# A two-layer expert network behind an attention: where the late weight conversions stand

## The chip, the cores and the metric
One core of a Trainium2 chip. The metric is the device time of one execution in microseconds (us), the median of several runs. TensorE does the matmuls (PE; its weight loads are shown as PEld), VectorE is DVE, ScalarE is ACT, GpSimd is POOL. SyncE (SP) issues all DMAs of this kernel, one after the other in program order.

## The reference, cut to what matters
All arithmetic is in float32; the matmuls have float32-like precision.

```
a     = softmax of phi (8, 8, 576, 32) over the 576 positions
k_m   = a^T k,  v_m = a^T v            # (8, 8, 32, 64): 32 memory slots per head
attn  = softmax(q k_m^T / 8)           # p: 576 x 32 per head
x     = attn v_m, heads side by side   # 4608 tokens x 512
h     = x @ w_in1;  g = h - tanh(h);   x = g @ w_out1      # 512 -> 2048 -> 512
h     = x @ w_in2;  g = h > 0 ? h : exp(min(h, 0)) - 1;  out = g @ w_out2
```

The four weight matrices arrive as 64-bit floats. The kernel turns them into float32 itself, and splits each value into a high and a low part, so that three matmuls (high x high, high x low, low x high) give a product of float32 precision.

## The kernel before, in words
A weight matrix is cut into 8 pages of 256 of the 2048 inner features. `conv` (L574) converts half a page: it loads 512 KB of raw words into one of three raw buffers (L580, L583), waits some rounds, and runs `convert` (L40): ACT takes an absolute value (L48), DVE does two tensor_scalars (L50, L51) and two scalar_tensor_tensors (L54, L57), ACT copies the high part (L62) and POOL subtracts it for the low part (L64). Pages 0 to 3 of the first layer's w_in stay whole (no split). For the second layer the two parts go to a staging tile and are stored to DRAM (L605); the first layer's parts stay on chip.

`Staged` (L251) spreads generators over rounds. `round` steps every live generator once, and starts a new one every second round, from the deque `first` and, if that is empty, from `todo`. `half` steps only those that asked for it: a conversion's ACT step (L48) is put there. `drain` runs rounds until nothing is left.

The first layer runs in 64 blocks (L765). A block is one slice `sw` of four (two pages, that is 512 inner features) by one group of 288 tokens `n`. `ss` is the half of the slices: blocks 0 to 31 hold slices 0 and 1 (pages 0 to 3), blocks 32 to 63 slices 2 and 3 (pages 4 to 7). For each of its two pages a block does `h_unit` (L349, 12 matmuls at L357: p against vw), the tanh-like function on ACT, POOL and DVE (`g_a` to `g_d`), and two `x_unit`s (L396, 12 matmuls each at L405) that lag behind by a block and more. `vw` is v_m times w_in, remade for each pair of batches (`vw_whole` at L344 for whole pages, `vw_half` at L328 for split ones). Units of attention (`units`) are stepped beside the blocks until the last one is done; then the pool of `at1` closes and its space goes to `wt3`, `vw2` and `wt2`.

In each block `cv.round()` is called once per page (L831), so that one conversion starts per block; in blocks 0 to 6 and 26 to 30 it is called a second time per page (L853, L854), so that two start. `need` (L568) runs further rounds at once where a page is wanted that is not converted.

Weight pages of the first layer lie in four pools. In `wt0` and `wt1`, on the right side of the memory, w_in pages use tags wi0 and wi1 (one 8 KB tile with a high and a low half per partition; pages 0 to 3 use only the first half) and w_out pages 0 to 3 use wo0 and wo1. Pages 4 and 5 of w_in take the tiles of pages 0 and 1, pages 6 and 7 those of 2 and 3. w_out pages 4, 5 are in `wt2`, pages 6, 7 in `wt3`; both pools exist only after `at1` closes. The pages 4 to 7 are converted from block 24 on: w_in 4, 5 are put in front at block 24, w_out 4, 5 behind them when `at1` closes, w_in 6, 7 and w_out 6, 7 at block 28. The second layer's 32 conversions are in `todo` from block 15.

At block 60 `open_l2` (L706) drains the conversions, closes `wt1` and `wt0` and opens the second layer's pools in their place; its first x loads (`load_x`, L434, into three xr buffers), sums (`add_x`, L440) and weight loads (L721) are then issued in blocks 60 to 63 by the list `soon`. `wt2` is closed at block 62. The second layer follows (L466 and L508).

Of the kernel before, what the change touches and what calls it, by code (L numbers as in the profile page):

```python
# [8 lines left out]
F32 = mybir.dt.float32  # L9
F32R = mybir.dt.float32r  # L10
# [15 lines left out]
NSW = 4  # L26
# [265 lines left out]
class Moe1:  # L292
# [23 lines left out]
    def vw_half(self, vm, wi, pg, po):  # L316
        nc = self.nc
        pars = range(2)
        if po == 0:
            for par in pars:  # L320
                pool = self.vw2_p if self.vw2_p and par and pg // 2 % 2 else self.vw_p
                self.vw[par, pg] = [pool.tile([128, 2, 256], F32R, tag=f"vw{pg % 2}_{par}{t}", name="vw")
                                    for t in range(2)]
        ps = self.misc.tile([128, 2, 256], F32, tag="m", name="vw_ps")
        for kc in range(2):
            p = 2 * po + kc
            for i, (a, b) in enumerate(((0, 0), (0, 1), (1, 0))):
                nc.tensor.matmul(ps[:, kc], lhsT=vm[:, a, p, :], rhs=wi[:, b, p, :], start=(i == 0), stop=(i == 2))  # L328
        parts = [(ps[64 * par:64 * par + 64], *(t[64 * po:64 * po + 64] for t in self.vw[par, pg])) for par in pars]
        for src, hi, lo in parts:  # L330
            nc.scalar.activation(hi, src, ACTF.Copy)
        for src, hi, lo in parts:
            nc.vector.tensor_tensor(lo, src, r32(hi), op=ALU.subtract)  # L333

    def vw_whole(self, vm, wi, pg, par, slot):
        nc = self.nc
        pool = self.vw2_p if self.vw2_p and par and pg // 2 % 2 else self.vw_p
        hi, lo = self.vw[par, pg] = [pool.tile([128, 2, 256], F32R, tag=f"vw{pg % 2}_{slot}{t}", name="vw")
                                     for t in range(2)]
        ps = self.misc.tile([128, 2, 256], F32, tag="m", name="vw_ps")  # L340
        for kc in range(2):
            for po in range(2):
                p = 2 * po + kc
                nc.tensor.matmul(ps[64 * po:64 * po + 64, kc], lhsT=vm[:, p, 64 * par:64 * par + 64],  # L344
                                 rhs=wi[:, 0, p, :], start=True, stop=True)
        nc.scalar.activation(hi, ps, ACTF.Copy)
        nc.vector.tensor_tensor(lo, ps, r32(hi), op=ALU.subtract)

# [47 lines left out]
    def x_unit(self, sw, n, dm, wo, on_act):  # L396
        nc = self.nc
        ps = self.misc.tile([128, NB], F32, tag="m", name="x_ps")
        k = 0
        for i in range(2):  # L400
            pg = 2 * sw + i
            g = self.g[n, pg]
            for j in range(2):
                for a, b in ((0, 0), (1, 0), (0, 1)):
                    nc.tensor.matmul(ps, lhsT=wo[pg][:, a, j, 128 * dm:128 * dm + 128], rhs=g[:, b, j, :],  # L405
                                     start=(k == 0), stop=(k == 11))
                    k += 1
        if dm % 2 == 0:
            self.x2[sw, n, dm // 2] = self.x_p.tile([128, 2, NB], F32, tag="x", name="x")
        t = self.x2[sw, n, dm // 2]  # L410
        if on_act:
            nc.scalar.activation(t[:, dm % 2], ps, ACTF.Copy)  # L412
        else:
            nc.vector.tensor_copy(t[:, dm % 2], ps)
        if dm == 3:
            for i in range(2):
                del self.g[n, 2 * sw + i]
# [113 lines left out]
def moe_kernel(tc, q, k, v, phi, w1, w2, w3, w4, out):  # L531
    nc = tc.nc
    with ExitStack() as top, tc.manual_schedule():
# [12 lines left out]
        wt_p = {0: new(l1b, "wt0", 1, side="right")}  # L546
# [8 lines left out]
        vm, vms = {}, {}  # L555
# [6 lines left out]
            return vm[b // 2][:, 2 * g:2 * g + 2, 64 * (b % 2):64 * (b % 2) + 64]  # L562

        wi, wo = {}, {}
        part = lambda t, h, c: t[:, h].rearrange("p a f -> p (a f)")[:, 512 * c:512 * c + 512]
        converted = set()

        def need(kind, pg, with_units=False):  # L568
# [5 lines left out]
        def conv(layer, kind, pg, c, lead=2):  # L574

            w = {("i", 1): w1, ("o", 1): w2, ("i", 2): w3, ("o", 2): w4}[kind, layer]
            raw = raw_p.tile([128, 512], mybir.dt.int64, tag="raw", name="raw")
            if kind == "i":
                src = w.rearrange("(k p) f -> p k f", p=128)[:, 2 * c:2 * c + 2, 256 * pg:256 * pg + 256]
                nc.sync.dma_start(out=raw.rearrange("p (a f) -> p a f", a=2), in_=src)  # L580
            else:
                r0 = 256 * pg + 128 * c
                nc.sync.dma_start(out=raw, in_=w[r0:r0 + 128, :])  # L583
            for k in range(lead + 1):
                yield k == lead
            staged, whole = [], (layer, kind) == (1, "i") and pg < 4

            def dst():
                if layer == 1:
                    ws = wi if kind == "i" else wo  # L590
                    if c == 0:
                        pool = wt_p[pg // 2 % (2 if kind == "i" else NSW)]
                        shape = [128, 2, 4, 256] if kind == "i" else [128, 2, 2, 512]
                        ws[pg] = pool.tile(shape, F32 if whole else F32R, tag=f"w{kind}{pg % 2}", name="w1")
                    if whole:
                        return part(ws[pg], 0, c)
                    return part(ws[pg], 0, c), part(ws[pg], 1, c)
                staged.append(wst_p[0].tile([128, 2, 512], F32R, tag="wst", name="wst"))
                return staged[-1][:, 0], staged[-1][:, 1]

            yield from convert(nc, cv_p, cv_ps, raw, dst, whole)
            converted.add((layer, kind, pg, c))
            if layer == 2:
                yield
                nc.sync.dma_start(out=w_dram[kind][pg, :, :, 512 * c:512 * c + 512], in_=r32(staged[-1]))  # L605

        conv_pair = lambda layer, kind, pg: [conv(layer, kind, pg, c) for c in range(2)]
        conv_l1 = lambda kind, *pgs: [g for pg in pgs for g in conv_pair(1, kind, pg)]
# [13 lines left out]
        cv = Staged([conv(1, "i", 1, 1)] + conv_l1("o", 0, 1), 2)  # L622
# [142 lines left out]
        for bi, (ss, bp, sub, j) in enumerate(blocks):  # L765
# [30 lines left out]
            if at1_open and 2 * B - 1 in p_done:  # L796
                at1_ctx.close()
                at1_open = False
                wt_p[3] = new(l1c, "wt3", 1)
                m1.vw2_p = new(l1c, "vw2", 1)  # L800
                wt_p[2] = new(late_ctx, "wt2", 1)
                cv.first.extend(conv_l1("o", 4, 5))
            if bi == 15:
                cv.todo.extend(conv_l2)
            if bi == 24:
                cv.first.extendleft(reversed(conv_l1("i", 4, 5)))
            if bi == 28:
                cv.first.extend(conv_l1("i", 6, 7) + conv_l1("o", 6, 7))
            if ss == 1 and j == 0 and sub == 1 and bp + 1 < B // 2 or bi == 28:
                load_vm((bp + 1) % (B // 2))  # L810
                vm_split = (bi + 1, (bp + 1) % (B // 2))
# [2 lines left out]
            for i in range(2):  # L814
                pg = 2 * sw + i
# [34 lines left out]
                x_next(bi < 22)  # L850
                m1.g_c(n, pg)
                cv.half()
                if bi < 7 or 26 <= bi < 31:  # L853
                    cv.round()  # L854
                    cv.half()
                units.round()
# [66 lines left out]
```

## Time and profile before
| | |
|---|---|
| median of 3 runs | 1709.38 us (1705.76 to 1710.95) |
| profiled execution | 1713.89 us, of it 1712.1 span |
| PE busy | 1613.9 us, 94% of the span |
| VectorE, ScalarE, GpSimd busy | 1187.0 us (69%), 931.0 us (54%), 757.2 us (44%) |
| granted TensorE clock, mean | 0.971 |

The span is the time from the first to the last instruction that the profile shows. Busy shares are means over stages that have different limits: the first layer ends at about 894 us, and behind it PE is hardly ever idle. A granted clock of 1.00 is 2.4 GHz and 0.5 is 1.2 GHz.

### The profile page before, as it was taken

The numbers are of one execution on the slowest core, as the hardware profiler recorded it, in microseconds if no ns is written. First come the engines' busy times: TensorE is split into PE (matmuls) and PEld (weight loads), VectorE is DVE, ScalarE is ACT, GpSimd is POOL, SyncE is SP. The second block draws the span as 40 slices with busy tenths as digits, with TensorE's granted clock in tenths as the row PEclk, the third lists the DMA queues.
The fourth block names the chain that finished last, engine by engine and source line by source line (L and its number), as shares of the span: only waits on it lengthen the run. The fifth ranks groups of instructions, "written<-read, shape, count | busy, mean of one in ns | idle before, by whom it ended". The sixth has DMA issues, their size and how long they took to land.

```text
span 1712.1 us, 26572 instructions
## 1 busy us (share of the span) xinstructions
PE 1613.9 (94%) x9884; PEld 1394.7 (81%) x9884; DVE 1187.0 (69%) x1730; ACT 931.0 (54%) x1677; POOL 757.2 (44%) x540
## 2 busy tenths in 40 slices
PE   5578999999989999999989999999999999999998
PEld 3346888787888999999989988888888888888886
DVE  4776767677989999999865655556555655565654
ACT  2455767677778888889853333333333333333332
POOL 1145655566666776767742222222222222222222
PEclk8668999999999999999999999999999999999999
DMA  8756566566565556666579321212121212121000
GB/s 194 213 172 179 176 188 198 182 201 226 192 212 176 170 193 219 220 214 215 182 238 360 103 62 48 74 49 63 49 74 42 70 50 74 50 65 59 25 14 25
DMA packets 140921, 236.09 MB, mean 138 GB/s; under 512 B 8184, under 2 KB 102392, under 8 KB 138744
## 3 DMA queue, kind: packets, MB, share of 16 engines
q1 hardware_dynamic: 140792, 234.39, 42.9%
q8 instruction: 78, 1.28, 0.3%
q14 instruction: 51, 0.42, 0.1%
HBM read 158.73 MB, written 74.45 MB: 136 GB/s over the span
## 4 chain that ended last, share of the span: by engine, by line
PE 65%; DVE 4%; DMA 4%; ACT 2%; issue 2%; POOL 1%; DVEq 0%; ACTq 0%; SPq 0%; POOLq 0%
PE h_ps L466 23%; PE o_ps L508 23%; PE x_ps L405 11%; PE h_ps L357 6%; PE vw_ps L328 1%; DMA p<-p_dram 1%; DMA xr<-x_dram 1%; DMA x_dram<-x 1%; DMA raw<-in_moe_w_in_dram 1%; DVE s L385 1%; DVE vw L333 1%; DVE h_ps L384 1%; ACT t L368 0%; DVE s L386 0%; POOL g L393 0%
## 5 line engine op out<-in xcount | busy, mean ns | idle before, releaser
L405 PE MATMUL x_ps<-g,w 128*128 128x288 f32 x3072 | 442.5, 297 | 11.8 <-POOL w L64 4.7
L492 POOL TENSOR_TENSOR e<-hm,e 128x512 fp32r<-128x512 f32 x144 | 187.1, 1299 | 576.9 <-ACT e L491 529.2
L405 PEld LDWEIGHTS x_ps<-g,w 128*128 128x128 f32 x3072 | 418.6, 189 | 25.6 <-ACT x L412 6.5
L466 PE MATMUL h_ps<-x,wi 128*128 128x512 f32 (+1 forms) x1920 | 424.6, 371 | 0.0
L508 PE MATMUL o_ps<-wo,e 128*128 128x512 f32 x1728 | 422.8, 393 | 0.7 <-POOL e L492 0.7
L466 PEld LDWEIGHTS h_ps<-x,wi 128*128 128x128 f32 x1920 | 336.1, 188 | 68.0
L508 PEld LDWEIGHTS o_ps<-wo,e 128*128 128x128 f32 x1728 | 323.4, 188 | 75.3 <-POOL e L492 1.1
L477 ACT ACTIVATE t_ps<-hm 128x512 f32<-128x512 f32 x144 | 86.7, 602 | 505.7 <-DVE hm L476 505.7
L375 POOL TENSOR_TENSOR v<-t,u 128x576 f32<-128x576 f32 x128 | 183.6, 1434 | 177.9 <-ACT u L369 161.1
L357 PE MATMUL h_ps<-p,vw 128*128 128x288 f32 x1536 | 240.2, 307 | 12.6 <-DVE s L386 6.6
L357 PEld LDWEIGHTS h_ps<-p,vw 128*128 128x128 f32 x1536 | 219.2, 196 | 24.5 <-issue 20.5
L483 DVE SCALAR_TENSOR_TENSOR hm<-hm,t_ps 128x512 f32<-128x512 f32 x144 | 99.1, 688 | 200.3 <-ACT hm L478 200.3
L393 POOL TENSOR_TENSOR g<-s,g 128x576 fp32r<-128x576 f32 x128 | 199.0, 1555 | 78.8 <-ACT g L392 71.5
L476 DVE TENSOR_SCALAR hm<-h_ps 128x512 f32<-128x512 f32 x144 | 99.6, 692 | 129.9 <-PE h_ps L466 129.2
L385 DVE SCALAR_TENSOR_TENSOR s<-s,v 128x576 f32<-128x576 f32 x128 | 137.3, 1073 | 7.3 <-POOL v L375 7.2
L368 ACT ACTIVATE t<-h_ps 128x576 f32<-128x576 f32 x128 | 83.3, 651 | 91.1 <-PE h_ps L357 38.8
L386 DVE COPY_PREDICATED s<-big,h_ps 128x576 f32<-128x576 uint32 x128 | 106.6, 833 | 12.8 <-ACT x L412 0.5
L370 ACT ACTIVATE s<-u,bias 128x576 f32<-128x576 f32 x128 | 99.5, 778 | 25.1 <-POOL g L393 15.5
L484 DVE SCALAR_TENSOR_TENSOR hm<-hm,t_ps 128x512 f32<-128x512 f32 x144 | 99.0, 688 | 5.0
L485 DVE TENSOR_TENSOR hm<-hm,h_ps 128x512 f32<-128x512 f32 x144 | 98.9, 687 | 5.0
L384 DVE TENSOR_TENSOR h_ps<-h_ps,t 128x576 f32<-128x576 f32 x128 | 96.6, 755 | 2.8 <-ACT u L369 2.7
L478 ACT ACTIVATE hm<-hm 128x512 f32<-128x512 f32 x144 | 91.0, 632 | 13.1
(88 smaller groups left out, 1681.2 us busy)
## 6 DMA issues: line engine op xcount, KB each, us to landing
x_dram<-x SPq DMA_DIRECT2D x128, 288.0 KB
xr<-x_dram SPq DMA_DIRECT2D x72, 512.0 KB
p<-p_dram SPq DMA_DIRECT2D x62, 576.0 KB
raw<-in_moe_w_in_dram SPq DMA_DIRECT2D x32, 512.0 KB
raw<-in_moe_w_out_dram SPq DMA_DIRECT2D x32, 512.0 KB
w_dram<-wst SPq DMA_DIRECT2D x32, 512.0 KB
kv<-in_k_dram SPq DMA_DIRECT2D x16, 576.0 KB
kv<-in_v_dram SPq DMA_DIRECT2D x16, 576.0 KB
```

The source lines that it names most:

```text
L357: nc.tensor.matmul(ps[:, j, :NB], lhsT=vw[a][:, kc, 128 * j:128 * j + 128], rhs=p[:, kc, b, :], start=(k == 0), stop=(k == 5))
L370: nc.scalar.activation(s, u, ACTF.Square, bias=bias[:, 0:1], scale=G_S)
L375: nc.gpsimd.tensor_tensor(v, t, u, op=ALU.mult)
L384: nc.vector.tensor_tensor(d, d, t, op=ALU.subtract)
L385: nc.vector.scalar_tensor_tensor(s, s, G_B, v, op0=ALU.add, op1=ALU.mult)
L386: nc.vector.copy_predicated(s, big.bitcast(U32), d)
L393: nc.gpsimd.tensor_tensor(g[:, 1], s, r32(g[:, 0]), op=ALU.subtract)
L405: nc.tensor.matmul(ps, lhsT=wo[pg][:, a, j, 128 * dm:128 * dm + 128], rhs=g[:, b, j, :], start=(k == 0), stop=(k == 11))
L466: nc.tensor.matmul(out, lhsT=w3[:, a, kc, 128 * j:128 * j + 128], rhs=x[:, b, kc, :], start=(i == 0), stop=(i == 11))
L476: nc.vector.tensor_scalar(hm, w[0], 0.0, None, op0=ALU.min)
L492: nc.gpsimd.tensor_tensor(e[:, 1], hm, r32(e[:, 0]), op=ALU.subtract)
L508: nc.tensor.matmul(acc, lhsT=e[:, a, jj, 128 * tg:128 * tg + 128], rhs=w4[:, b, j, :], start=(k == 0 and jj == 0 and i == 0), stop=(k == l ...
```

## The change
The tiles of the first layer's weights become halves of 4 KB per partition, and the halves that the whole w_in pages left unused get a tag of their own. The high parts of w_in pages 4 to 7 still take the places of pages 0 to 3; their low parts go to `wt2`. w_out page 4 goes to the two spare halves in `wt0` (tags wi0b, wi1b), page 5 to those in `wt1`; pages 6, 7 stay in `wt3`. So w_out 4, 5 no longer have to wait for `at1` to close: they are put into `todo` at block 8. The second layer's conversions are put there at block 12. When `at1` closes, w_out 6, 7 are put into `first`; at block 28 w_in 6, 7 go in front of them. The second call of `cv.round()` in blocks 26 to 30 goes away.

```
-                nc.tensor.matmul(ps[:, kc], lhsT=vm[:, a, p, :], rhs=wi[:, b, p, :], start=(i == 0), stop=(i == 2))
+                nc.tensor.matmul(ps[:, kc], lhsT=vm[:, a, p, :], rhs=wi[b][:, p, :], start=(i == 0), stop=(i == 2))
...
                     if c == 0:
-                        pool = wt_p[pg // 2 % (2 if kind == "i" else NSW)]
-                        shape = [128, 2, 4, 256] if kind == "i" else [128, 2, 2, 512]
-                        ws[pg] = pool.tile(shape, F32 if whole else F32R, tag=f"w{kind}{pg % 2}", name="w1")
+                        pg2, odd = divmod(pg, 2)
+                        if kind == "i":
+                            ws[pg] = [wt_p[pg2 % 2].tile([128, 4, 256], F32 if whole else F32R, tag=f"wi{odd}a", name="w1")]
+                            if not whole:
+                                ws[pg].append(wt_p[2].tile([128, 4, 256], F32R, tag=f"wl{pg}", name="w1"))
+                        else:
+                            pool, tags = (wt_p[odd], "wi0b wi1b") if pg2 == 2 else (wt_p[pg2], f"wo{odd}a wo{odd}b")
+                            ws[pg] = [pool.tile([128, 2, 512], F32R, tag=t, name="w1") for t in tags.split()]
...
                 wt_p[2] = new(late_ctx, "wt2", 1)
-                cv.first.extend(conv_l1("o", 4, 5))
-            if bi == 15:
+                cv.first.extend(conv_l1("o", 6, 7))
+            if bi == 8:
+                cv.todo.extend(conv_l1("o", 4, 5))
+            if bi == 12:
                 cv.todo.extend(conv_l2)
             if bi == 24:
                 cv.first.extendleft(reversed(conv_l1("i", 4, 5)))
             if bi == 28:
-                cv.first.extend(conv_l1("i", 6, 7) + conv_l1("o", 6, 7))
+                cv.first.extendleft(reversed(conv_l1("i", 6, 7)))
...
                 cv.half()
-                if bi < 7 or 26 <= bi < 31:
+                if bi < 7:
                     cv.round()
                     cv.half()
```

## Rows read from the trace of the kernel before

**Rows 1.** Busy time by stage (start:end, length, busy with count, clock, DMA share, GB/s)
```profile
237.70:340.70 103.00, 97.61 (x813) 84.06 (x812) 70.80 (x111) 72.19 (x143) 60.04 (x44) 1.00 0.63 191
340.70:474.30 133.60, 126.26 (x1023) 112.20 (x1022) 106.42 (x163) 102.48 (x199) 86.27 (x60) 1.00 0.65 210
474.30:552.70 78.40, 70.36 (x491) 65.79 (x490) 69.95 (x102) 61.13 (x108) 50.18 (x37) 0.93 0.58 187
552.70:594.30 41.60, 41.40 (x315) 41.20 (x314) 39.05 (x57) 37.18 (x66) 29.65 (x20) 1.00 0.52 173
594.30:844.50 250.20, 249.14 (x1874) 247.90 (x1873) 234.44 (x337) 222.02 (x387) 177.57 (x123) 1.00 0.59 209
844.50:883.70 39.20, 31.86 (x219) 31.32 (x217) 23.89 (x28) 22.94 (x40) 19.86 (x13) 0.91 0.69 184
```

**Rows 2.** L48 from 205 to 480 us: count, shortest/median/longest, first and last
```profile
L48 ACT ACTIVATE cv_m<-raw x11: 618/637/662, 347.3 to 479.9; 128x512 f32<-128x512 f32 x11
```

**Rows 3.** SP in order of time, the last store of attention
```profile
457.96 0.33 SPq L231 DMA_DIRECT2D p_dram<-phl  x1
```

**Rows 4.** VectorE's groups from 340.7 to 840: busy, mean ns, idle before
```profile
L50 DVE TENSOR_SCALAR cv_m<-cv_m 128x512 f32<-128x512 f32 x48 | 33.6, 700 | 3.4 <-ACT cv_m L48 2.9
L54 DVE SCALAR_TENSOR_TENSOR cv_m<-raw,cv_m 128x512 uint32<-128x512 uint32 x48 | 33.5, 697 | 0.6
```

**Rows 5.** Busy time by block: blocks 10, 26, 27, 60, 61, 62
```profile
252.90:268.80 15.90, 14.87 (x142) 12.88 (x140) 13.34 (x23) 10.73 (x22) 9.97 (x8) 1.00 0.55 188
474.30:486.20 11.90, 11.90 (x91) 10.52 (x89) 10.57 (x15) 10.36 (x19) 8.58 (x8) 1.00 0.68 213
486.20:503.90 17.70, 13.01 (x91) 10.89 (x89) 15.08 (x23) 10.87 (x20) 8.67 (x7) 0.90 0.64 206
844.50:854.10 9.60, 9.60 (x74) 9.60 (x73) 6.90 (x9) 8.01 (x14) 7.56 (x5) 1.00 0.48 152
854.10:870.50 16.40, 9.80 (x74) 9.60 (x73) 7.22 (x10) 5.65 (x11) 4.58 (x4) 0.96 0.57 153
870.50:883.70 13.20, 12.46 (x73) 12.12 (x73) 9.76 (x10) 9.28 (x17) 7.73 (x5) 0.79 1.00 246
```

**Rows 6.** Chain that ended last: start, us; two transfers on it
```profile
483.96 13.67 DMA raw<-in_moe_w_in_dram
...
868.44 15.12 DMA p<-p_dram
```

**Rows 7.** Timeline of block 27: start, us, [idle before <- what ended it]
```profile
497.72 0.62 ACT L48 ACTIVATE cv_m<-raw 128x512 f32<-128x512 f32 x1 [4.64 <-DMA raw<-in_moe_w_in_dram]
...
501.95 1.97 PE L344 MATMUL vw_ps<-w,vm 128*64 128x256 f32 x8 [4.01 <-ACT x L412]
```

**Rows 8.** What L48 waited for from 560 to 840 us (us, times), whole list
```profile
  DVE cv_a L57: 9.3, 9
```

**Rows 9.** SP in order of time, blocks 59 to 61
```profile
839.05 9.88 SPq L605 DMA_DIRECT2D w_dram<-wst  x2
...
849.63 0.88 SPq L434 DMA_DIRECT2D xr<-x_dram  x1
...
854.18 14.17 SPq L434 DMA_DIRECT2D xr<-x_dram  x2
```

**Rows 10.** Busy time and DMA share in block 60, three us
```profile
846.00:849.00 3.00, 3.00 (x25) 3.00 (x24) 2.13 (x3) 2.75 (x6) 3.00 (x3) 1.00 0.00 0
```

**Rows 11.** Timeline of block 61, its end
```profile
866.58 1.23 DVE L440 TENSOR_TENSOR xr<-xr 128x1024 f32<-128x1024 f32 x1 [8.73 <-DMA xr<-x_dram]
...
870.50 3.22 PE L357 MATMUL h_ps<-p,vw 128*128 128x288 f32 x12 [6.60 <-DVE s L386]
```

**Rows 12.** L385 from 163 to 311 us and from 340 to 455
```profile
L385 DVE SCALAR_TENSOR_TENSOR s<-s,v x19: 742/759/1630, 171.1 to 304.4; 128x576 f32<-128x576 f32 x19
...
L385 DVE SCALAR_TENSOR_TENSOR s<-s,v x16: 741/757/1930, 339.3 to 449.8; 128x576 f32<-128x576 f32 x16
```

**Rows 13.** PE's waits from 0 to 250 us: total, times, longest
```profile
PE x_ps L405 <- POOL w L64: 4.7, 2, 2.4
```

More of the change, by code (lines that the diff above doesn't have):

```diff
@@ L344, in vw_whole @@
                 nc.tensor.matmul(ps[64 * po:64 * po + 64, kc], lhsT=vm[:, p, 64 * par:64 * par + 64],
-                                 rhs=wi[:, 0, p, :], start=True, stop=True)
+                                 rhs=wi[0][:, p, :], start=True, stop=True)
         nc.scalar.activation(hi, ps, ACTF.Copy)
@@ L404, in x_unit @@
                 for a, b in ((0, 0), (1, 0), (0, 1)):
-                    nc.tensor.matmul(ps, lhsT=wo[pg][:, a, j, 128 * dm:128 * dm + 128], rhs=g[:, b, j, :],
+                    nc.tensor.matmul(ps, lhsT=wo[pg][a][:, j, 128 * dm:128 * dm + 128], rhs=g[:, b, j, :],
                                      start=(k == 0), stop=(k == 11))
@@ L564, in moe_kernel @@
         wi, wo = {}, {}
-        part = lambda t, h, c: t[:, h].rearrange("p a f -> p (a f)")[:, 512 * c:512 * c + 512]
+        part = lambda t, c: t.rearrange("p a f -> p (a f)")[:, 512 * c:512 * c + 512]
         converted = set()
@@ L591, in dst @@
                     if c == 0:
-                        pool = wt_p[pg // 2 % (2 if kind == "i" else NSW)]
-                        shape = [128, 2, 4, 256] if kind == "i" else [128, 2, 2, 512]
-                        ws[pg] = pool.tile(shape, F32 if whole else F32R, tag=f"w{kind}{pg % 2}", name="w1")
+                        pg2, odd = divmod(pg, 2)
[6 more added lines that the diff above has]
+                            ws[pg] = [pool.tile([128, 2, 512], F32R, tag=t, name="w1") for t in tags.split()]
                     if whole:
-                        return part(ws[pg], 0, c)
-                    return part(ws[pg], 0, c), part(ws[pg], 1, c)
+                        return part(ws[pg][0], c)
+                    return [part(t, c) for t in ws[pg]]
                 staged.append(wst_p[0].tile([128, 2, 512], F32R, tag="wst", name="wst"))
```

## The prediction
> **What bounds the kernel now.** I read busy time by stage first, then single blocks, then the waits and the chain inside the blocks that are long. Blocks are the 64 block steps of the first layer, each found by its 24 L357 matmuls. TensorE (PE) is the busiest engine in every stage [rows 1], so the reader is to look for the stretches where it idles: only they can give time back, and only new ones can cost any. In blocks 36 to 59 (594.3 to 844.5) PE idles 250.2 - 249.14 = 1.1 us, with one conversion per block. In blocks 26 to 31 (474.3 to 552.7) it idles 8.0 us, and its granted clock averages 0.93. In blocks 60 to 62 (844.5 to 883.7) it idles 7.3 us at 0.91. In blocks 9 to 15 it idles 5.4 us, and there the kernel before runs no conversion: after 205 us the first L48 starts at 347.3 [rows 2]. The change touches exactly these stretches: conversions leave 26 to 31, enter 9 to 15, and are finished earlier before block 60.
>
> **Rounds, counted from the code.** One conversion starts every second round. Its six steps are, at two rounds a block: load at the first round of block b, Abs (L48) at the first half of b+1, two tensor_scalars, two scalar_tensor_tensors, the copy, and the GpSimd subtract at the first round of b+3. With the two extra rounds a block of 26 to 30, two start per block, and load and Abs are three quarters of a block apart instead of a block and a quarter. The last unit of attention issues its store at 457.96 [rows 3], in block 24 (455.2 to 464.8), so at1 closes at block 25 in both. Before: blocks 16 to 25 one conversion each, 26 to 30 two each, then one each; the last (w_out page 7, layer 2) is left for the drain at block 60. After: w_out 4, 5 start in 8 to 11 and are done in 14; layer 2 from 12; one per block throughout; the last store comes in block 58 and the drain is empty. The number of conversions is the same; seven come into 9 to 15, five leave 26 to 30, three leave 56 to 58, one is forced into 37.
>
> **Price of one conversion.** On VectorE 2 x 0.700 (L50, and L51 like it) and 2 x 0.697 (L54, and L57 like it) [rows 4]: 2.79 us.
>
> **Term 1, blocks 26 to 31: -11.5 us.** They take 78.4 us. What they must take: block 26 runs with PE never idle in 11.9, and 27 has the same matmuls (16 of L344); 28 to 31 hold the same work as 32 to 35, two plain blocks and two with L328, which take 41.6 [rows 1, 5]. So 2 x 11.9 + 41.6 = 65.4, and at most 13.0 can be gained. Two things cause the loss. First, a load that comes too late for the doubled pace: the w_in load issued at 483.96 took 13.67 us [rows 6]; ScalarE sat idle for its last 4.64, the x_ps copy behind it came late, and PE waited 4.01 us [rows 7], after which part of the block ran at the lower clock level, 1.2 GHz (0.90 in the mean of block 27 [rows 5]). Second, VectorE is full: 69.95 of 78.4 busy. The five conversions that leave take 5 x 2.79 = 14.0 us off it, and the load's lead grows to a block and a quarter, 12 to 15 us. That this lead is enough at one per block, with more traffic (209 GB/s against 187), is shown by blocks 32 to 59: there L48 waited only for the previous conversion's VectorE steps, never for a load [rows 8, 1]. Bounds: the wait in block 27 might stay; 27 then keeps 17.7 - 11.9 = 5.8 [rows 5] and the gain is 7.2. Above is 13.0. A loss has no cause here, since work only leaves. I take 11.5, near the upper end, since blocks 32 to 59 are the nearest row.
>
> **Term 2, blocks 60 to 62: -6 us.** SyncE (SP) issues in order. The drain's second w_dram store waits for its GpSimd subtract, so SP stands in L605 from 839.05 to 848.9; the DMA engines run dry (share 0.00 from 846 to 849) and the x store, two xr loads and a p load are issued late and together. VectorE then waits 8.7 us at L440 for an xr load, which holds back the release of h_ps: PE waits 6.6 us [rows 9 to 11]. Block 61 takes 16.4 and 62, partly at the lower clock, 13.2, where a plain block takes 9.6 (block 60) [rows 5]: 10.4 us above the floor. After, the store is gone. The first xr load and p (1.1 MB) can go out at about 845, five us earlier, into the empty stretch; the second xr load waits for an x_ps copy anyway. It landed at about 866.5; the five transfers from 849 to its end (two x, two xr, a p, 2.2 MB) went at 0.126 MB/us. At this pace, all of them begun at 845 end at 862; with the first xr and the p done by 849, the 0.8 MB up to its end are there at 855. L440 wants it at 866.58 - 8.73 = 858. So the wait of 8.7 becomes 0 to 4. What is late next: the p load for block 63, queued on SP behind the xr load that waits for L440. It was issued at 868.44 and took 15.12 us [rows 6] beside weight loads; issued at 858 to 863 it lands at 873 to 878, and block 63 wants it at 844.5 + 3 x 9.6 = 873.3. Block 63 then starts 5 to 10 us earlier than 883.7. Bounds: 10.4, and 0 if the DMA queues stay as crowded; below nothing, see the third rival. I take 6; the second layer behind it moves along as a whole.
>
> **Term 3, blocks 9 to 15: +3 us.** Seven conversions come in beside attention. If all their VectorE time were on the path: 7 x 2.79 = 19.5. If they filled idle time: 0. The nearest row is 340.7 to 474.3, ten blocks with attention and one conversion each: PE idle 0.73 per block, against 0.77 in 9 to 15 without any [rows 1]. No gain is possible, since work only comes in. So about nothing; but attention is denser here: block 10 has VectorE 13.34 of 15.9 busy, and 13.34 + 2.79 is just over its length [rows 5]. I take 3, nearer to the row that says nothing. The added load per block stands in SP's queue in front of q, kv and p loads, which are issued blocks ahead; I price that at nothing, and within the 3 if that cover is gone.
> The Trainium skill, "SBUF — State Buffer", section "Who interferes with whom", speaks against this part: a VectorE instruction with two SBUF inputs and a GpSimd instruction that reads SBUF shut each other out for a whole instruction. The trace shows the lengthening itself, at L385, but with the same median without conversions (0.759, up to 1.63) as with them (0.757, up to 1.93) [rows 12]. What it would cost is the fifth rival.
>
> **Term 4, block 37: +1 us.** The last w_out page of the first layer now starts in block 35 and is forced by one round when the first x_unit of slice 3 asks for it; PE then waits for a GpSimd subtract. The trace has two such waits, in block 3, of up to 2.4 us [rows 13]. Bounds 0 and 2.4; I take 1. After that the steps stand half a block later in 38 to 55, where VectorE is 94% busy: within 1 us either way. Edits at nothing: the tiles split in halves change no instruction; 56 to 58 get lighter where PE had no idle time to give.
>
> **Sum.** -11.5 - 6 + 3 + 1 = -13.5. The profiled execution took 1713.9 (span 1712.1), 4.5 above the median of 1709.4; on the median: 1695.9, so 1696.
>
> **Rivals.**
> 1. The transition gains nothing, since weight and xr loads crowd the queues anyway (DMA share 1.00 in block 62 [rows 5]): -11.5 + 4 = -7.5, 1702. Against it: the queues were empty just before. 0.13.
> 2. Block 27's wait stays, made by traffic that doesn't leave (p, x, the last layer-2 stores): -7.2 - 6 + 4 = -9.2, 1700. 0.08.
> 3. Pages 4, 5 now lie in pools closed at block 60 while the x_units of block 59 still read them until block 61. If a tile loaded there lies over them, SP waits for those units, until about 862 (the third x_unit of block 61: five sixths of 9.6 behind 854.1) instead of 849.6: +12.4 in place of a gain, with -11.5 + 4 that is +4.9, 1714. By the order of the pools the xr buffers lie over the raw buffers and w_in pages, the page tiles at the pools' ends. 0.05.
> 4. Slower: in blocks 9 to 15 VectorE's order decides. Each conversion's 2.79 goes ahead of the g_c steps that free h_ps, and nothing absorbs it: +19.5, and the transition as before: -11.5 + 19.5 + 1 = +9, 1718. It decides where a block's VectorE time exceeds its length, as in block 10; the average, 70.8 of 103.0, plus 19.5, [rows 1], speaks against it. 0.06.
> 5. GpSimd's seven added subtracts meet L385: 7 x (1.93 - 0.757) = 8.2 on top of the sum, -5.3 in all: 1704. 0.06.
> 6. Both gains at their ends, no cost: -13.0 - 10.4: 1686. 0.04.
> My forecast has 0.58 and by itself 1690 to 1702. The range 1687 to 1706 leaves out the fourth rival, the third, the sixth and the edge of the fifth, less than 2 in 10. A measurement here tells no change from 0.3%, 5.1 us: faster means below 1704.3. That is nearly all of the forecast, most of rivals 1 and 2, half of 5, and 6: 0.80; within 0.3% 0.12; slower 0.08.
>
> **What would show it.** Term 1: 26 to 31 take 65 to 68 us, no L48 waits for a raw load, the clock stays at 1.00. Term 2: no L605 on SP after block 58, L440 waits under 4 us, 61 and 62 together under 24 us. Term 3: 9 to 15 take 103 to 108 us, with seven L48 among them. Term 4: a PE wait for L64 near block 37. I am wrong if 9 to 15 lengthen by over 10 us, or if 60 to 62 stay at 39 us.

## The result and the profile after

The changed kernel takes 1732.88 us in the median of 4 runs (1729.33 to 1736.99), the kernel before 1708.93 beside it: the ratio is 1.0133 (95% interval 1.0115 to 1.0152). It is 1.3% slower, where 0.8% faster was forecast. The profiled execution took 1733.28 us, 1731.5 of it span, with a mean granted clock of 0.969. The span of before was 1712.1, so 19.4 us have to be found. The medians lie 24.0 us apart; the other 4.6 come from the profiled execution of before, which was about 5 us longer than the median of its kernel, and the blocks can't show them.

The first view is busy time by stage in the changed kernel. The cuts stand at the starts of the same blocks as in [rows 1], with the stage after block 31 cut finer: blocks 9 to 15, 16 to 25, 26 to 31, 32 to 36, 37 and 38, 39 to 56, 57 to 60, 61 and 62. The columns are those of [rows 1].

```profile
234.20:342.30 108.10, 99.23 (x812) 84.96 (x812) 90.03 (x137) 78.56 (x156) 67.91 (x49) 0.98 0.72 214
342.30:478.60 136.30, 128.54 (x1024) 113.06 (x1022) 109.15 (x165) 103.16 (x200) 88.39 (x62) 0.99 0.66 216
478.60:545.50 66.90, 65.92 (x489) 62.50 (x490) 60.24 (x82) 55.49 (x97) 43.67 (x32) 1.00 0.55 173
545.50:596.50 51.00, 51.00 (x387) 50.79 (x386) 48.53 (x71) 44.95 (x79) 35.43 (x25) 1.00 0.56 176
596.50:624.80 28.30, 23.60 (x158) 23.16 (x158) 19.78 (x29) 19.77 (x35) 17.27 (x13) 0.88 0.48 155
624.80:819.20 194.40, 189.62 (x1406) 186.19 (x1405) 186.82 (x254) 168.70 (x291) 128.02 (x92) 1.00 0.61 204
819.20:860.50 41.30, 41.30 (x313) 41.23 (x314) 33.23 (x42) 33.81 (x59) 25.89 (x19) 1.00 0.35 123
860.50:903.00 42.50, 21.29 (x146) 20.66 (x145) 17.23 (x19) 15.44 (x27) 12.58 (x9) 0.76 0.61 146
```

Blocks 26 to 31 gave back what was forecast: 66.9 us against 78.4, at a clock of 1.00. Blocks 61 and 62 hold the worst loss: PE is busy for 21.29 of 42.50 us. The second new hole is blocks 37 and 38 (PE idle 4.7 us, clock 0.88). The third is spread out: blocks 39 to 56 take 194.4, with VectorE busy for 186.82 of it.

The table gives the same sums, in us, for the profiled execution of every kernel, each worked out from the starts of the L357 groups in its trace. It is what all the experiments below are read from.

```
                0-8   9-15 16-25 26-31 32-36 37-38 39-56 57-60 61-62 63-end   span
before         172.2 103.0 133.6  78.3  51.2  20.6 188.0  41.6  29.5  828.4 1712.1
after          170.0 108.1 136.3  66.9  51.0  28.3 194.4  41.3  42.5  828.5 1731.5
e1_pools       167.8 106.9 135.8  65.5  51.1  28.9 194.6  41.3  22.1  828.4 1705.9
e2_early       173.7 106.0 135.4  65.3  51.1  20.6 188.1  41.2  42.7  828.4 1715.0
e12_both       172.0 108.2 137.4  65.4  51.1  20.7 188.1  41.2  20.7  829.1 1697.7
e3_l2_at14     173.1 102.0 137.6  78.9  50.9  20.6 187.7  41.3  20.6  829.1 1705.5
e4_l2_at8      170.5 107.0 135.6  81.4  50.9  20.6 187.2  41.3  24.5  828.2 1710.6
e8_phase       172.1 103.0 133.6  77.6  51.2  20.6 195.3  42.6  25.5  829.3 1715.7
e9_start9      168.9 105.9 138.3  65.4  51.1  20.7 188.3  41.2  22.5  828.4 1694.4
e6_pace        169.8 108.3 136.8  76.3  50.8  20.6 187.1  41.1  22.5  828.4 1707.8
e10_two        170.8 102.9 136.8  76.8  51.2  24.2 193.0  41.7  25.3  828.4 1714.9
e13_phase9     170.3 108.8 135.6  66.3  53.5  21.1 195.4  41.3  21.5  829.1 1705.5
```

From before to after, the start of block 0 and blocks 0 to 8 make -3.5 us, 9 to 15 +5.1, 16 to 25 +2.7, 26 to 31 -11.4, 37 and 38 +7.7, 39 to 56 +6.4, 61 and 62 +13.0, the rest -0.4: +19.4, up to rounding. Each line is one execution, and three columns scatter where the code is the same. Up to block 36, e8_phase and e10_two have the order of before, and yet their blocks 16 to 25 take 133.6 and 136.8; so the +2.7 there is not shown to come from the change. Up to block 22 after, e1_pools, e2_early, e12_both and e6_pace have the same order, and their blocks 9 to 15 take 106.0 to 108.3, against 102.9 to 103.0 in the three kernels without conversions there (before, e8_phase, e10_two). So a cost is there in every one of them, but it lies between 3 and 5.4. Blocks 0 to 8 scatter by 6 us.

**Blocks 61 and 62.** SP in order of time, in the changed kernel (start, us until it was done, how often). The last w_dram store is not in it; it was issued at 830.0, in block 58, as forecast.

```profile
844.15 5.87 SPq L420 DMA_DIRECT2D x_dram<-x  x2
868.47 0.59 SPq L434 DMA_DIRECT2D xr<-x_dram  x1
869.11 0.54 SPq L313 DMA_DIRECT2D p<-p_dram  x1
...
871.59 15.78 SPq L434 DMA_DIRECT2D xr<-x_dram  x2
887.43 0.56 SPq L313 DMA_DIRECT2D p<-p_dram  x1
```

The first xr load was to go out at 845. It goes out at 868.47, and p, queued behind it, at 869.11. [rows 9] had it at 849.63. What it waited for, and what VectorE and PE waited for from 855 to 905 (us in total, times, longest):

```profile
SPq L434 <- PE x_ps L405: 18.5, 1, 18.5
...
DVE xr L440 <- DMA xr<-x_dram: 21.1, 1, 21.1
...
PE h_ps L357 <- DVE s L386: 20.1, 2, 19.4
```

And the timeline of the same place (idle time before, and what ended it, in brackets), which answers to [rows 11]:

```profile
866.82 3.34 PE L405 MATMUL x_ps<-g,w 128*128 128x288 f32 x24
...
885.60 1.23 DVE L440 TENSOR_TENSOR xr<-xr 128x1024 f32<-128x1024 f32 x1 [21.11 <-DMA xr<-x_dram]
...
889.53 3.22 PE L357 MATMUL h_ps<-p,vw 128*128 128x288 f32 x12 [19.37 <-DVE s L386]
```

The first twelve of the 24 matmuls at 866.82, done at about 868.5, are the last x_unit of block 59, and that is the last reader of w_out page 5. The built program's memory map says why a load of x waits for it: xr's first buffer takes bytes 167,904 to 172,000 of each partition, and so does the low part of page 5 (tag wi1b in `wt1`). The other two xr buffers lie over the raw buffers, which nothing reads any more. The right-side pools grow downwards from the top of the memory; I had laid them out from the other end.

**Blocks 37 and 38.** Timeline of block 37 in the changed kernel:

```profile
606.52 0.69 DVE L57 SCALAR_TENSOR_TENSOR cv_a<-raw,cv_m 128x512 uint32<-128x512 uint32 x1
606.90 0.61 ACT L62 ACTIVATE w<-cv_a 128x512 fp32r<-128x512 f32 x1
...
607.57 0.40 PE L405 MATMUL x_ps<-g,w 128*128 128x288 f32 x1 [1.82 <-ACT w L62]
...
608.17 1.40 POOL L393 TENSOR_TENSOR g<-s,g 128x576 fp32r<-128x576 f32 x1 [0.49 <-ACT g L392]
609.52 1.26 POOL L64 TENSOR_TENSOR w<-cv_a,w 128x512 fp32r<-128x512 f32 x1
...
610.84 0.85 PE L405 MATMUL x_ps<-g,w 128*128 128x288 f32 x2 [2.87 <-POOL w L64]
```

Not only the GpSimd subtract is late: the forced round leaves the end of the conversion (L57, L62, L64, one behind the other on three engines) right in front of the matmuls that read the page, and on GpSimd L393 still stands ahead of L64. PE stops twice, 4.7 us in all, block 37 takes 15.0 in place of 9.6, and block 38 runs at a mean clock of 0.81, part of it thus at 1.2 GHz, and takes 13.3 in place of 11.0.

**Blocks 39 to 56.** The 36 L385 of these blocks: first before, then after (count, shortest/median/longest in ns, first and last start).

```profile
L385 DVE SCALAR_TENSOR_TENSOR s<-s,v x36: 746/954/1971, 625.1 to 810.1; 128x576 f32<-128x576 f32 x36
```

```profile
L385 DVE SCALAR_TENSOR_TENSOR s<-s,v x36: 747/1460/2005, 626.0 to 816.7; 128x576 f32<-128x576 f32 x36
```

Count and shape are the same; the median went from 954 to 1460 ns. More below, at e8_phase.

### The profile page after: what moved, and what is told of

Its sections match the earlier page's. It is cut to its first block, busy times and chain, and to the rows that moved or that the text cites. A ratio compares the mean times of both kernels' runs of the same rounds, so it can differ in the third digit from the quotient of the medians.

```text
span 1731.5 us, 26542 instructions
## 1 busy us (share of the span) xinstructions
PE 1616.3 (93%) x9884; PEld 1393.6 (80%) x9884; DVE 1207.1 (70%) x1730; ACT 932.2 (54%) x1677; POOL 752.0 (43%) x540
## 4 chain that ended last, share of the span: by engine, by line
PE 65%; DVE 5%; ACT 2%; DMA 2%; issue 2%; POOL 1%; SPq 0%; DVEq 0%; ACTq 0%; POOLq 0%
PE h_ps L466 23%; PE o_ps L508 23%; PE x_ps L405 12%; PE h_ps L357 6%; DVE s L385 2%; PE vw_ps L328 1%; DMA p<-p_dram 1%; DMA xr<-x_dram 1%; DVE h_ps L384 1%; DVE vw L333 1%; DVE s L386 1%; PE vw_ps L344 0%; DVE x L414 0%; ACT big L379 0%; DVE cv_m L54 0%
## 5 line engine op out<-in xcount | busy, mean ns | idle before, releaser
L357 PE MATMUL h_ps<-p,vw 128*128 128x288 f32 x1536 | 239.2, 306 | 26.4 <-DVE s L386 20.1
L357 PEld LDWEIGHTS h_ps<-p,vw 128*128 128x128 f32 x1536 | 217.3, 195 | 40.3 <-issue 34.2
L393 POOL TENSOR_TENSOR g<-s,g 128x576 fp32r<-128x576 f32 x128 | 193.0, 1508 | 86.5 <-ACT g L392 77.1
L385 DVE SCALAR_TENSOR_TENSOR s<-s,v 128x576 f32<-128x576 f32 x128 | 156.8, 1225 | 5.8 <-POOL v L375 5.8
L379 ACT ACTIVATE big<-u,bias 128x576 f32<-128x576 f32 x128 | 98.1, 766 | 0.7 <-DVE s L386 0.4
```

The costliest lines, as they stand in the source:

```text
L357: nc.tensor.matmul(ps[:, j, :NB], lhsT=vw[a][:, kc, 128 * j:128 * j + 128], rhs=p[:, kc, b, :], start=(k == 0), stop=(k == 5))
L385: nc.vector.scalar_tensor_tensor(s, s, G_B, v, op0=ALU.add, op1=ALU.mult)
L393: nc.gpsimd.tensor_tensor(g[:, 1], s, r32(g[:, 0]), op=ALU.subtract)
```

## The experiments

Theory A: three separate mishaps were added, and apart from them the forecast mechanisms hold. The first xr buffer lies over page 5 (61 and 62); the forced round stalls PE (37 and 38); and the half block by which it moves all later conversions sets L385 against GpSimd (39 to 56). Rivals, B: the DMA traffic of the new schedule, or simply more VectorE work earlier, is the cause.

### e1_pools: the second layer's pools in another order

```
             m2.xr_p = pool("xr", 3)      # after;  here: e, ew, xr, xs
             m2.x_p = [pool("xs", 1)]
             m2.ew = pool("ew", 2)
             m2.e_p = pool("e", 3)
```

> The changed kernel, with the second layer's first four pools opened in another order (e, ew, xr, xs instead of xr, xs, ew, e), so that the tiles first written, the xr buffers, no longer lie over w_out page 5 in the pool of w_in pages; nothing else. Theory A: the first xr load stands on SyncE until the last x_unit of block 59 has read page 5 (18.5 us of waiting in the changed kernel), and this alone makes blocks 61 and 62 take 42.5 us. Then SyncE's wait for TensorE at the xr loads is gone, block 61 and 62 together take 20 to 24 us, below the 29.6 of the kernel before, since no w_dram store stands in the way either: 13 to 22 us below the changed kernel, 1711 to 1720. Rival: the transfers crowd each other wherever they start. Then VectorE still waits 8 us or more for an xr load, 61 and 62 take 29 to 42 us, and the time is 1720 to 1733.

Measured: 1708.05 us, ratio to before 0.9983 (0.9966 to 1.0001), below the 1711 to 1720 expected. Blocks 61 and 62 fall from 42.5 to 22.1, as expected. SP in order of time in this kernel, where block 60 begins at 845.8 and block 61 at 855.3:

```profile
844.95 0.59 SPq L434 DMA_DIRECT2D xr<-x_dram  x1
845.63 0.54 SPq L313 DMA_DIRECT2D p<-p_dram  x1
...
850.46 0.57 SPq L434 DMA_DIRECT2D xr<-x_dram  x1
```

The first xr load goes out ahead of block 60's start, its wait for the x_units is gone, and L440 waits for xr for 0.2 us in all. In this program's memory map the first xr buffer starts at byte 151,520, over the low part of a w_out page of the first half, which is no longer read; page 5's low part now lies under an e buffer. The conversions, traffic and tiles are the same: the address alone made the hole. Block 37 (15.6 us) and 39 to 56 (194.6) stay as in after, so these are something else.

### e2_early: the w_in pages 4 to 7 one block sooner

```
-            if bi == 24:
+            if bi == 23:
                 cv.first.extendleft(reversed(conv_l1("i", 4, 5)))
-            if bi == 28:
+            if bi == 27:
                 cv.first.extendleft(reversed(conv_l1("i", 6, 7)))
```

> The changed kernel, with w_in 4, 5 put in front at block 23 instead of 24 and w_in 6, 7 at block 27 instead of 28, so that every later conversion of the first layer starts one block earlier and w_out page 7 is ready in block 37 without a forced round; nothing else. Theory A: the forced round costs the stall in block 37 with the lower clock behind it (15.0 + 13.3 us instead of 9.6 + 11.0: 7.7 us) and, because it shifts every later conversion by half a block, the slower blocks 39 to 56 (194.4 us instead of 188.0: 6.4 us). Both go: 14 us below the changed kernel, about 1719; blocks 61 and 62 stay at 42 us. Rival: 39 to 56 are slow for another reason (the place of the tiles, the low parts in another pool): only the 7.7 go, about 1725, and 39 to 56 still take 194 us.

Measured: 1717.12 us, ratio 1.0045 (1.0030 to 1.0061). No round is forced any more. Blocks 37 and 38 take 20.6 and 39 to 56 take 188.1, both as before; 61 and 62 keep their hole (42.7). So both losses go with the forced round; what the shift alone costs is taken up at e8_phase.

### e12_both: both edits

The edits of e1_pools and e2_early together.

> Both edits at once: the other order of pools, and w_in 4, 5 and 6, 7 one block earlier. If the two causes are independent, the gains add: 1733 - 14 - (13 to 22), that is 1697 to 1706, faster than the kernel before by 3 to 12 us; what is left against the plan is the price of the seven conversions in blocks 9 to 15 (108.1 us instead of 103.0 in the changed kernel). Rival: what is gained in 37 to 56 is waited for at the second layer's start: 1709 or above.

Measured: 1697.73 us, ratio 0.9920 (0.9893 to 0.9948), below before and 2 us above the time that was forecast for the change itself. Span 1697.7. Blocks 26 to 31 take 65.4 (-12.9), 61 and 62 20.7 (-8.8), 9 to 15 108.2 (+5.2), 16 to 25 +3.8; all others together -1.5. The parts add up to the 14.4 us of span, up to rounding, and what remains of cost lies in blocks 9 to 25.

### e3_l2_at14: before, with the layer-2 conversions put in one block sooner

```
-            if bi == 15:
+            if bi == 14:
                 cv.todo.extend(conv_l2)
```

With this one edit the drain at block 60 has nothing left to do; no tile is changed.

> The kernel before, with the second layer's conversions put into the queue at block 14 instead of 15, so that the last one is stored in block 59 and the drain at block 60 is empty; nothing else. Theory A (my step for blocks 60 to 62): SyncE's stand of 10 us at the drain's stores makes the first xr loads late; without it blocks 61 and 62 take 20 to 25 us instead of 29.6, the time falls by 4 to 9 us, 1700 to 1705. Rival: the loads land late for their own number; 29 us again, 1707 to 1711.

Measured: 1705.53 us, ratio 0.9972 (0.9961 to 0.9984), just above the 1700 to 1705 expected. SP in order of time here:

```profile
840.97 0.56 SPq L605 DMA_DIRECT2D w_dram<-wst  x1
844.89 0.37 SPq L420 DMA_DIRECT2D x_dram<-x  x1
845.31 0.58 SPq L434 DMA_DIRECT2D xr<-x_dram  x1
845.99 0.56 SPq L313 DMA_DIRECT2D p<-p_dram  x1
```

The L605 that stood 9.88 us in [rows 9] takes 0.56, the xr load goes out at 845.31, and blocks 61 and 62 take 20.6 in place of 29.5. That is the mechanism of Term 2, alone, and 8.9 us where 6 was forecast. Blocks 16 to 25 took 4.0 more in the profiled execution, by blocks 18 and 19 (18.4 and 20.4, against 16.7 and 18.6 before); e10_two, with the order of before in these blocks, has 18.1 and 20.4 there as well, so this is scatter.

### e4_l2_at8: before, with conversions in blocks 9 to 15

```
-            if bi == 15:
+            if bi == 8:
                 cv.todo.extend(conv_l2)
```

> The kernel before, with the second layer's conversions put into the queue at block 8 instead of 15; tiles, pools and the double pace of 26 to 30 as before. So seven conversions come into blocks 9 to 15 without any change of tiles, and the drain at block 60 is empty. Theory A (the conversions themselves cost what the changed kernel lost there): 9 to 15 take 107 to 109 us instead of 103.0, 16 to 25 take 136 to 138 instead of 133.6, and 61 and 62 about 21 instead of 29.5; in all about 1 us below the kernel before, 1708 to 1712. Rival: the loss in 9 to 15 came from the divided tiles and their places: 103 us, and the time is 1702 or below.

Measured: 1711.51 us, ratio 1.0001 (0.9990 to 1.0012). Busy time of blocks 9 to 15 in this kernel:

```profile
236.10:343.10 107.00, 97.57 (x812) 83.89 (x811) 89.14 (x137) 79.17 (x158) 66.10 (x48) 1.00 0.76 234
```

With the tiles as before, the seven conversions cost 4.0 us here (107.0 against 103.0): the conversions themselves, not the split tiles, make Term 3. Blocks 26 to 31 are no better for it (81.4). Blocks 61 and 62 took 24.5 where about 21 was expected, though the drain was empty here too; where the 3.5 us went was not followed up.

### e6_pace: both edits, and the double pace of blocks 26 to 30 again

```
-                if bi < 7:
+                if bi < 7 or 26 <= bi < 31:
                     cv.round()
                     cv.half()
```

> Both edits, and the second call of a round put back into blocks 26 to 30, so that two conversions start in each of them again (the second layer then ends five blocks earlier). Theory A: the pace itself makes these blocks slow, by loads that come too late and by a full VectorE: 26 to 31 take 74 to 79 us instead of 65.4, and the time rises by 8 to 13 us to 1706 to 1711. Rival: they were slow for what else was moved out of them (w_out 4, 5 and their place): 65 to 68 us, 1698.

Measured: 1707.36 us, ratio 0.9983 (0.9970 to 0.9997). Blocks 26 to 31 are back at 76.3. Busy time of block 27 and of 26 to 31 there, and what ACT waited for from 492.9 on:

```profile
492.90:508.70 15.80, 12.06 (x91) 10.54 (x89) 12.73 (x21) 9.97 (x18) 8.06 (x6) 1.00 0.61 187
481.00:557.30 76.30, 69.45 (x491) 65.52 (x490) 68.55 (x102) 61.08 (x107) 50.71 (x37) 0.96 0.59 185
```

```profile
ACT cv_m L48 <- DMA raw<-in_moe_w_out_dram: 3.9, 1, 3.9
ACT cv_m L48 <- DMA raw<-in_moe_w_in_dram: 2.3, 1, 2.3
```

The waits of L48 for a raw load come back with the pace (in after, L48 waited for no load in blocks 26 to 31), and VectorE is again at 90%. The pace alone is worth 10.9 us of these blocks and 9.6 us of the median. How much of it is the late loads and how much the full VectorE isn't separated.

### e8_phase: before, with one extra round at block 37

```
+                if bi == 37 and i == 1:
+                    cv.round()
```

It stands in front of the block's last x_unit; nothing waits for a conversion there. It moves all later conversions by half a block, and leaves one round less for the drain at block 60.

> The kernel before with one more round of conversions in block 37, in front of its last x_unit, where nothing waits for it; so all later conversions stand half a block later in their blocks, with no stall to begin with. Theory A: the place of the steps within the block costs: blocks 39 to 56 take 194 us instead of 188.0, while 37 and 38 together stay under 22 us (the changed kernel: 28.3). Rival: the slow blocks were a consequence of the stall or of the tiles: 39 to 56 stay at 188. The drain at block 60 gets one round shorter too, so 61 and 62 may gain up to 9 us: the total lies between 1706 and 1717, and the blocks decide.

Measured: 1715.33 us, ratio 1.0035 (1.0022 to 1.0049). Blocks 37 and 38 take 20.6, with no stall; 39 to 56 take 195.3 against 188.0. For these blocks follow, of before and then of this kernel, the busy time, the L385 group of VectorE (busy, mean ns, idle before), and PE's wait for vw:

```profile
624.50:812.50 188.00, 187.00 (x1407) 186.00 (x1405) 177.70 (x253) 166.94 (x291) 132.04 (x92) 1.00 0.62 217
```

```profile
L385 DVE SCALAR_TENSOR_TENSOR s<-s,v 128x576 f32<-128x576 f32 x36 | 40.3, 1120 | 0.0
```

```profile
PE vw_ps L328 <- DVE vw L333: 0.9, 3, 0.5
```

```profile
623.00:818.30 195.30, 189.65 (x1406) 186.35 (x1405) 187.38 (x254) 169.46 (x293) 128.86 (x92) 1.00 0.62 212
```

```profile
L385 DVE SCALAR_TENSOR_TENSOR s<-s,v 128x576 f32<-128x576 f32 x36 | 48.7, 1352 | 0.0
```

```profile
PE vw_ps L328 <- DVE vw L333: 5.3, 8, 1.1
```

VectorE issues the same instructions and is busy 9.7 us longer, 8.4 of it in L385. It was at 94.5% of the stage before, so there was little to take this up: the stage is 7.3 longer, and PE waits 4.4 us more for VectorE's vw. The rest of the 7.3 shows for the most part as longer busy time of PE (189.65 against 187.00). One such place in the timeline of e8_phase:

```profile
710.80 0.78 DVE L385 SCALAR_TENSOR_TENSOR s<-s,v 128x576 f32<-128x576 f32 x1
...
710.93 1.97 POOL L393 TENSOR_TENSOR g<-s,g 128x576 fp32r<-128x576 f32 x1
...
716.58 1.43 POOL L393 TENSOR_TENSOR g<-s,g 128x576 fp32r<-128x576 f32 x1 [1.50 <-ACT g L392]
716.62 2.00 DVE L385 SCALAR_TENSOR_TENSOR s<-s,v 128x576 f32<-128x576 f32 x1
...
720.96 0.94 PE L328 MATMUL vw_ps<-w,vms 128*128 128x256 f32 x6 [1.10 <-DVE vw L333]
```

L385 that starts 0.13 us ahead of GpSimd's L393 takes 0.78 (and L393 takes 1.97); L385 that starts 0.04 us behind it takes 2.00. Counted over the 36 in the trace of each: with no GpSimd instruction running at its start L385 took 0.75 us every time (15 of 36 before, 9 here, 9 in after); with one running it took 0.75 to 2.01. L393 was that one 13 times before, 23 times here and 23 times in after. The other kernels fall into the same two groups: with the half block, e1_pools 23 and e13_phase9 22 times, with 39 to 56 at 194.6 and 195.4 us; without it, e2_early 13 and e12_both 14 times, at 188.1 us in both. That the shift costs the 7.3 us is shown; that it does so by L385's place against L393 is read from these rows, and no run moved that pair alone.

### e10_two: before, with two extra rounds at block 37

```
+                if bi == 37:
+                    cv.round()
```

One for each page: a whole block's shift, so that the steps stand where they stood.

> The kernel before with two more rounds of conversions in block 37, one for each of its pages, where nothing waits for them; so one conversion comes a whole block earlier and the steps keep their places within the block. Theory A: it is the place within the block that costs (with one more round 39 to 56 took 195.3 us, and the line L385 1352 ns in the mean against 1120): with two, 39 to 56 take 187 to 189 us, L385 about 1130 ns. Rival: any conversion pulled forward costs, or the changed order of the queue: 192 us or more. The drain at block 60 is empty as well, so 61 and 62 take 20 to 26 us instead of 29.5: 1702 to 1708 in all.

Measured: 1706.24 us, ratio 0.9982 (0.9964 to 1.0000): no loss in the median, as theory A has it, against e8_phase's 1.0035, though the shorter drain gives something back in it too. L385's mean in blocks 39 to 56 is 1053 ns, so it is not lengthened. The block sums of the profiled execution don't fit, though: 24.2 in 37 and 38, and 193.0 in 39 to 56. That execution took 1716.74, nearly the longest of ten (1702.89 to 1716.80), so its sums are not those of the median. By them the rival (192 us or more) is not ruled out. In it, from 600 to 830 us, ACT's L62 waited 9.8 us for the w_dram stores and PE 2.4 for p loads, which neither theory had said. L385 speaks for A, and the median too, but less sharply; what a whole block's lead costs in the longest executions stays open.

### e9_start9: both edits, conversions from block 9 on

```
-            if bi == 8:
+            if bi == 9:
                 cv.todo.extend(conv_l1("o", 4, 5))
-            if bi == 12:
+            if bi == 13:
                 cv.todo.extend(conv_l2)
```

> Both edits (pools in the other order, w_in 4, 5 and 6, 7 one block earlier), and w_out 4, 5 from block 9 and the second layer from block 13, one block later each; the last store then comes in block 59. Theory: what 9 to 15 lose is lost where a conversion's VectorE steps meet attention's in block 10 (18.7 us instead of 15.9). One conversion less in 9 to 15, and block 10 with two VectorE steps fewer: 9 to 15 take 105 to 107 instead of 108.2, the time is 1 to 3 us below 1698. Rival: the loss only moves to the block behind: 108, and 1698.

Measured: 1697.62 us, ratio 0.9919 (0.9894 to 0.9943), against 0.9920 of e12_both: no difference. Blocks 9 to 15 take 105.9 in place of 108.2, but e2_early has 106.0 with all seven conversions, and 16 to 25 take 138.3 in place of 137.4. The 1 to 3 us expected didn't come: one conversion less in the dense blocks doesn't lower the time.

### e13_phase9: both edits, the steps of blocks 9 to 25 moved by half a block

```
+                if bi in (8, 25) and i == 1:
+                    cv.round()
```

> Both edits (pools in the other order, w_in 4, 5 and 6, 7 one block earlier), with one more round of conversions in block 8 and one more in block 25, so that between them the steps stand half a block later in their blocks, and from 26 on as before. Theory: also beside attention the price of a conversion is set by where its VectorE steps fall, in 10 (18.7 us instead of 15.9), 18 and 19 (39.0 instead of 35.3); 9 to 25 take another time than the 245.6 us of the kernel with both edits, by 3 us or more to either side, below it if the steps miss the places where TensorE waits for attention's VectorE steps. Rival: the price is that of the engines' filling and the same anywhere: 244 to 247 us, and the same time, 1696 to 1700.

Measured: 1707.47 us, ratio 0.9989 (0.9974 to 1.0004). It didn't test what it was for. The queue runs empty at block 11, so the first shift is lost at block 12, and the second, meant to undo it, stays until the end. Blocks 9 to 25 take 244.4 in place of 245.6, which tells nothing, and 39 to 56 take 195.4 with L385 at 1357 ns: a second showing, by accident, that the half-block place costs 7 us there. Whether another place would lower Term 3 is open.

## Why the prediction was wrong

The forecast was 1696 (1687 to 1706), and the time 1732.88.

Of the 32.9 us by which the spans miss the sum (+19.4 for -13.5), 19.0 belong to Term 2 and 13.1 to Term 4; Term 3 and blocks 16 to 25 have 2.1 and 2.7, and the start with blocks 0 to 8 gave 3.5 back, which is within its scatter.

**Term 1, -11.5: right.** 26 to 31 took 66.9 where 65 to 68 was forecast, the clock stood at 1.00, and L48 waited for no raw load. In e1_pools, e2_early, e12_both and e9_start9 they took 65.3 to 65.5, the floor of 65.4 that the forecast had worked out. e6_pace shows the cause that was given: with the double pace, the waits and the 76.3 return.

**Term 2, -6: the mechanism was right, the step that failed is the free passage of the first xr load.** The step read "The first xr load and p (1.1 MB) can go out at about 845". In after SP stood 18.5 us in front of it. This was the third rival, "If a tile loaded there lies over them, SP waits for those units, until about 862", with a chance of 0.05. It was put down by "the xr buffers lie over the raw buffers and w_in pages, the page tiles at the pools' ends", which is a layout I worked out from the wrong end of the memory. The address of one 4 KB buffer decided 20 us (42.5 against 22.1 in e1_pools), and it could be known from the order and the sizes of the pools. The rival had the right unit and the right price: +12.4. Block 61 began 6.4 us later than before (860.5 against 854.1), so the unit ended at 868.47 and not at 862; less these 6.4 the xr load went out 12.4 us later than before, PE stood 19.37 us in place of 6.60 [rows 11], and the two blocks took 13.0 more. What its 1714 lacked is for the most part Term 4; its own fault was the chance of 0.05. Without the overlap the term is worth -8.9 (e3_l2_at14) and -8.8 (e12_both), and -7.0 to -7.4 in e1_pools, e6_pace and e9_start9: more than 6.

**Term 3, +3: right sign, too small.** 9 to 15 took 108.1, +5.1, at the upper end of the 103 to 108 named; e4_l2_at8 shows 4.0 without the tile change. The worst block is 10, with 18.3 us in place of 15.9 [rows 5]; it scatters from 16.6 to 18.8 in the kernels with the same order there. In the timeline of e12_both, VectorE in block 10:

```profile
262.99 0.68 DVE L50 TENSOR_SCALAR cv_m<-cv_m 128x512 f32<-128x512 f32 x1
...
263.70 0.70 DVE L51 TENSOR_SCALAR cv_m<-cv_m 128x512 uint32<-128x512 uint32 x1
...
264.96 0.59 DVE L172 TENSOR_SCALAR vbd<-km,rs,pmask 128x64 f32<-128x64 f32 x2
...
265.69 0.27 PE L127 MATMUL mT<-ident,cmax 96*128 96x96 f32 x1 [2.06 <-DVE vbd L172]
```

Two conversion steps stand in front of attention's L172, and PE waits 2.06 us for it (1.9 in after, and no such wait in block 10 before). That is akin to the fourth rival (VectorE's order decides, and in block 10), but the step kept waiting is attention's and not the g_c steps that the rival named, and it is one block and not seven.

The next largest is block 14, with 12.1 us in place of 10.7 in all five kernels with that order, and it is no matter of VectorE. GpSimd and PE there, in the changed kernel:

```profile
315.03 1.29 POOL L64 TENSOR_TENSOR w<-cv_a,w 128x512 fp32r<-128x512 f32 x1
316.30 1.11 POOL L133 TENSOR_SCALAR dmax<-ident,nmax 128x128 f32<-128x128 f32 x1
...
317.45 0.46 PE L136 MATMUL bmax<-dmax,ones 128*96 128x128 f32 x2 [1.14 <-POOL dmax L133]
```

A conversion's GpSimd subtract stands in front of attention's L133, and PE waits 1.14 us; before, with no conversion there, no such wait is in block 14. GpSimd's order beside attention was in no term of the sum. L385, the fifth rival, was not the reason named for either wait.

**Term 4, +1: the step failed twice.** "PE then waits for a GpSimd subtract", 0 to 2.4: it waited for ACT's L62 as well, and block 38 paid by its clock, +7.7. [rows 13] was a wait for the last step alone; here the forced round put the last steps together in front of PE, and it paid for L62 (1.82) and for L64 (2.87), and then by the clock. The other sentence, "After that the steps stand half a block later in 38 to 55, where VectorE is 94% busy: within 1 us either way", cost +6.4; e8_phase, with that and a drain one round shorter, shows 7.3 in these blocks. The Trainium skill, "SBUF — State Buffer", section "Who interferes with whom", has the rule for it: who issues first holds the shared port for its whole instruction, so the order of issue decides. The trace agrees, with L385 at 0.78 ahead of L393 and 2.00 behind it. The prediction used the rule for the seven added subtracts of Term 3 and not for the shift, where no instruction is added at all.

**The sum.** The bounds of Terms 2 and 4 were each too narrow by a case that the text had named: the overlap with a chance of 0.05, the shift at 1 us. With both taken out (e12_both) the span falls by 14.4, close to the -13.5 forecast. That closeness is in part luck: Terms 1 and 2 gave 1.4 and 2.8 more than forecast, Term 3 cost 2.2 more, and blocks 16 to 25 took 3.8 that no term had.

## What to carry to other kernels

Where a change moves tiles, work out the byte addresses of whatever is later loaded in their place, pool by pool and from the right end, and look for the last reader of these bytes: with loads issued in order, one such wait holds back every load behind it. Where a change moves steps by a part of a period, an engine that is 94% busy has little room for a worse pairing; the difference between the shortest and the longest of the instruction concerned, times its count, bounds the price (here 1.25 us times 36, 45 us, of which 8.4 came). When a conversion is forced at the moment of its use, look at every step of its chain that PE may wait for, and at the clock behind it: here 1.82 and 2.87 us of waits, and 2.3 us in the block that followed.

## What was not expected of the hardware

VectorE's L385 takes 0.75 us with no GpSimd instruction running at its start (every one of 15 before and of 9 in after) and up to 2.01 with one; started 40 ns behind L393 it took 2.00, and 0.13 us ahead of it 0.78. And half a block in the place of the conversions, with no instruction added, moved its mean over 36 from 1120 to 1352 ns and the stage by 7.3 us.
